# Strassen's seven products in the first MLP layer of three of four row blocks

## The chip, the core and the metric

The kernel runs on one core of a Trainium2 chip. The metric is the device time of one execution, in microseconds (us), as the median of several runs of the same program.

## The reference

The kernel mixes two branches over a sequence of 2048 rows of width 512, all in f32. The first is a linear attention with learned softmax features; the second is a two-layer MLP with a Mish between.

```python
g = sigmoid((x * gate_w).sum(-1, keepdims=True))
# a: 32 heads of 16; features = softmax(+-(head @ w_phi)), concatenated
qkv = x @ wqkv
phi_q, phi_k = features(q), features(k)
num = phi_q @ (phi_k.T @ v);  den = phi_q @ phi_k.sum(rows) + 1e-6
a = (num / den) @ wo
# b: hidden width 1376
h = x @ w1 + b1
b = (h * tanh(softplus(h))) @ w2
out = g * a + (1 - g) * b
```

## The kernel before, in words

Every f32 matmul that matters is done as three matmuls in the format `fp32r`: an operand is split into a high half (a rounded copy, made on ScalarE) and a low half (the difference, made on GpSimd or VectorE), and high·high, high·low and low·high are summed in PSUM.

The work has two stages. In the first, eight chunks of 256 rows go through the projections `k`, `v`, `q` and through the features of `k`; q goes out to DRAM (`pqd`), and the MLP's weights are loaded piece by piece (`ldw`) and split (`wh`, `wl`) one chunk later. The second stage has four row blocks of 512 rows. In a block:

- `up` i computes one tile of 128 hidden units for the 512 rows: 12 matmuls of 512 columns (three terms, four k tiles). `mi` is Mish on ScalarE, `hi` and `lo` are the two halves of its result (`lo`, variable `l`, on GpSimd). There are 11 tiles; the first holds 96 hidden units and, as an extra column, the gate.
- `dn` i adds that tile's part of the second layer into four PSUM banks (12 matmuls of 512 columns); the last one is `df0` to `df3`, one for each 128 rows.
- `lq`, `mx`, `mn`, `d0`, `d1`, `E`, `S`, `T`, `rS`, `D`, `m`, `de`, `rd`, `sc`, `es`, `tr` are the attention features of one tile of 128 rows: a load, then VectorE instructions, with an exponential on ScalarE (`E`). `tr` writes to DRAM (`ed`), `mv` loads it back transposed (`eT`).
- `nu`, `oh`, `ol`, `wo`, `ag`, `fi` are the attention's product, its split, the output projection, the gate, and the sum that is stored.
- `LX`, `XH`, `XL` load and split the next block's x (`xbh`, `xbl`).

No scheduler reorders anything: the order of instructions on every engine is that of strings written by hand (`BLOCK0`, `BLOCK1`, `BLOCK` twice), a word for each step; a word with `+` belongs to the next block, with `'` to the previous one. Each engine works through its queue in that order, and a step waits only for the semaphores of its operands and of the buffers that it reuses. Nearly all DMAs are issued from SP's queue, in the same order. All PSUM tiles of `up`, `num` and half of `wo` share three banks.

In a block before, the attention of the next block's first two tiles runs well ahead, up to `tr1+`, and no VectorE instruction of the MLP stands between `up` and `dn`.

Of the kernel before, what the change touches and what calls it, by code (L numbers as in the profile page):

```python
# [8 lines left out]
F32 = mybir.dt.float32  # L9
# [5 lines left out]
P = 128  # L15
# [16 lines left out]
ORDER = [NFA - 1] + list(range(NFA - 1)) + list(range(NFA, NF))  # L32
WARM = 10
# [10 lines left out]
    S1 rS1 ml1 z1 ve1 q0 qe0 st0 q1 qe1 st1  # L44
# [4 lines left out]
    S1 rS1 ml1 z1 ve1 q0 qe0 st0 q1 qe1 st1 mx0+ mn0+ kv" kv' kv  # L49
# [3 lines left out]
    S1 rS1 ml1 z1 v1 ve1 q0 mx1+ mn1+ d01+ d11+ qe0 st0 q1 qe1 st1 E1+  # L53
# [3 lines left out]
    v1 ve1 mx2+ mn2+ XL1 q0 qe0 st0 q1 qe1 st1 zt zf zs S0+ zl kv' kv rS0+ km  # L57
# [5 lines left out]
    up0 lq3 mi0 gr hi0 lo0 ldo0 ldo1 S1 rS1 up1 up2 mi1 hi1 lo1 wh0 wl0 d02 d12 T0 D0 m0 de0 rd0 sc0 es0 tr0 mi2 hi2 up3 dn0 hc lo2  # L63
    mi3 hi3 lo3 T1 D1 m1 de1 rd1 sc1 es1 tr1 mv0 lq0+ lq1+ mx3 mn3 d03 d13 WH0 dn1
    up4 mi4 hi4 lo4 WH1 WL0 dn2 E2 S2 T2 rS2 D2 m2 de2 rd2 sc2 es2 tr2 up5 mi5 hi5 lo5 WL1 dn3 E3 ge gg up6 mi6 hi6 lo6 dn4
    up7 mi7 hi7 lo7 dn5 S3 T3 rS3 D3 m3 de3 rd3 sc3 es3 tr3 mv1 up8 mi8 hi8 lo8 dn6
    mx0+ mn0+ d00+ d10+ mx1+ mn1+ d01+ d11+ lq2+ lq3+ up9 mi9 hi9 lo9 dn7 E0+ E1+ S0+ T0+ LX0 rS0+ D0+ m0+ de0+ rd0+ sc0+
    up10 mi10 hi10 lo10 dn8 dn9 cd nu0 nu1 oh0 ol0 es0+ tr0+ XH0+ XL0+ S1+ T1+ rS1+ LX1 df0 df1 wo0 ag0 wo1 oh1 ol1 ag1 D1+ fi0
    m1+ de1+ rd1+ sc1+ df2 df3 wo2 ag2 fi1 XH1+ XL1+ es1+ fi2 wo3 ag3 fi3 tr1+ mv0+
"""  # L70
BLOCK1 = """
    up0 mi0 hi0 lo0 gr mx2 mn2 d02 d12 mx3 mn3 d03 d13 up1 mi1 hi1 lo1 lq0+ lq1+ E2 E3 hc S2 T2 rS2 D2 m2 de2 rd2 sc2 es2 tr2
    up2 mi2 hi2 lo2 dn0 S3 T3 rS3 D3 m3 de3 rd3 sc3 es3 tr3 mv1 up3 mi3 hi3 lo3 dn1 up4 mi4 hi4 lo4 dn2
    mx0+ mn0+ d00+ d10+ mx1+ mn1+ d01+ d11+ lq2+ lq3+ up5 mi5 hi5 lo5 dn3 E0+ E1+ ge gg
    S0+ T0+ rS0+ D0+ m0+ de0+ rd0+ sc0+ es0+ tr0+ up6 mi6 hi6 lo6 dn4 up7 mi7 hi7 lo7 dn5 cd nu0 nu1 oh0 ol0 S1+ T1+ rS1+ D1+ LX0 LX1
    m1+ de1+ rd1+ sc1+ es1+ dn6 wo0 ag0 wo1 ag1 oh1 ol1 tr1+ mv0+ dn7 up8 mi8 hi8 lo8 mx2+ mn2+ d02+ d12+ mx3+ mn3+ d03+ d13+
    wo2 ag2 up9 mi9 hi9 lo9 dn8 E2+ E3+ up10 mi10 hi10 lo10 wo3 ag3 XH0+ XL0+ XH1+ XL1+ dn9 df0 fi0 df1 fi1 df2 fi2 df3 fi3
"""
BLOCK = """
    up0 mi0 hi0 lo0 gr lq0+ lq1+ S2 T2 rS2 D2 m2 de2 rd2 sc2 es2 tr2 up1 mi1 hi1 lo1 hc up2 mi2 hi2 lo2 dn0  # L80
    S3 T3 rS3 D3 m3 de3 rd3 sc3 es3 tr3 mv1 up3 mi3 hi3 lo3 dn1 up4 mi4 hi4 lo4 dn2
    mx0+ mn0+ d00+ d10+ mx1+ mn1+ d01+ d11+ lq2+ lq3+ up5 mi5 hi5 lo5 dn3 E0+ E1+ ge gg
    S0+ T0+ rS0+ D0+ m0+ de0+ rd0+ sc0+ up6 mi6 hi6 lo6 dn4 cd nu0 nu1 oh0 ol0 es0+ tr0+ S1+ T1+ rS1+ D1+ LX0 LX1 m1+ de1+ rd1+ sc1+
    es1+ dn5 wo0 ag0 wo1 ag1 oh1 ol1 tr1+ mv0+ dn6 up7 mi7 hi7 lo7 wo2 ag2 mx2+ mn2+ d02+ d12+ mx3+ mn3+ d03+ d13+
    up8 mi8 hi8 lo8 dn7 E2+ E3+ up9 mi9 hi9 lo9 wo3 ag3 up10 mi10 hi10 lo10 dn8 XH0+ XL0+ XH1+ XL1+ dn9 df0 fi0 df1 fi1 df2 fi2 df3 fi3
"""
# [3 lines left out]
def tile_gated_mix(ctx: ExitStack, tc: tile.TileContext, xT, wv, wkT, wqT, bd, w1a, w1b, b1, w2a, w2b, wo, out):  # L90
# [324 lines left out]

    def x_ops(b, load, split):

        raw = {}
        for h in range(2):
# [9 lines left out]
            def xl(h=h):  # L429
                sl = slice(h * SC, (h + 1) * SC)  # L430
                pin(V.tensor_sub(xb[b][1][:, :, sl], kt(raw[h], SC), f32(xb[b][0][:, :, sl])))  # L431
# [3 lines left out]
            at(split, f"XL{h}", xl)  # L435

# [75 lines left out]
    def b_ops(b):  # L512
        key = ("B", b)
        U, dn, eTs, num, ohl, io, ed = {}, {}, {}, {}, {}, {}, {}

        def up(i):
            f = ORDER[i]
# [78 lines left out]
        at(key, "gr", gr)  # L596
        at(key, "ge", ge)
# [3 lines left out]
        for t in range(4):  # L601
# [290 lines left out]
```

## Time and profile before

| | |
|---|---|
| runs | 444.29, 444.42, 444.49 us; median 444.42 |
| profiled execution | span 442.5 us, 1.9 us under the median of the runs |
| TensorE / VectorE / ScalarE / GpSimd busy | 437.8 / 313.2 / 201.4 / 159.6 us |
| projections and start | 0 to 149.35 us |
| row blocks 1 to 4 | 149.35 to 221.98, to 294.34, to 366.75, to 439.20 us |
| moved by DMA | 49.64 MB, 112 GB/s on average |

In the profile, PE is TensorE's matmuls and PEld its weight loads, which overlap; DVE is VectorE, ACT ScalarE, POOL GpSimd, SP the engine that issues most DMAs. The duration of a matmul row is its latency, 0.39 us for 512 columns; the pace is read from the starts of neighbouring rows. The same holds for VectorE rows, whose ends overlap the next start by up to 0.1 us.

### The profile page before, as it was taken

The page shows a single profiled execution, that of the slowest core. Times are in us where ns is not written, and L with a number is a line of the kernel's source. Part 1 is how long each engine was busy: PE and PEld are TensorE (multiplying, and loading weights), DVE is VectorE, ACT ScalarE, POOL GpSimd, SP SyncE. Part 2 cuts the span into 40 slices and gives each one's busy share as a digit, 9 for nine tenths or more (in the row PEclk, how much of TensorE's full clock was granted, in tenths as well). Part 3 has the DMA queues.
Part 4 walks back from the last instruction along what each step waited for, and adds up shares of the span by engine and source line. Part 5 has one row for each costly group of instructions (what it writes and reads, how often), then busy time and mean ns, then how long its engine had stood idle before and what let it go on. Part 6 is the DMA issues. An engine that isn't in the chain of part 4 may idle for free.

```text
span 442.5 us, 7179 instructions
## 1 busy us (share of the span) xinstructions
PE 437.8 (99%) x2874; PEld 359.9 (81%) x2874; DVE 313.2 (71%) x420; ACT 201.4 (46%) x286; POOL 159.6 (36%) x100
## 2 busy tenths in 40 slices
PE   8999999999999999999999999999999999999996
PEld 7888888888888888887888878888878888887885
DVE  3987739559699999999999898279679329601103
ACT  3644523533345455736376533646352645341330
POOL 3078694785662453621024120215310222411121
PEclk9999999999999999999999999999999999999999
DMA  7721631524403136425362533222605302310002
GB/s 265 283 96 48 191 120 50 188 86 133 167 29 116 49 84 209 142 101 168 128 205 96 159 124 120 75 96 95 191 0 192 94 2 96 134 57 1 0 0 96
DMA packets 29001, 49.64 MB, mean 112 GB/s; under 512 B 6308, under 2 KB 15012, under 8 KB 28968
## 3 DMA queue, kind: packets, MB, share of 16 engines
q1 hardware_dynamic: 28648, 48.79, 32.9%
q8 instruction: 22, 0.36, 0.3%
q10 hardware_dynamic: 288, 0.39, 0.3%
q14 instruction: 11, 0.09, 0.1%
q0 software_dynamic: 32, 0.01, 0.0%
HBM read 31.73 MB, written 16.79 MB: 110 GB/s over the span
## 4 chain that ended last, share of the span: by engine, by line
PE 98%; DMA 1%; SPq 0%; DVE 0%; issue 0%
PE proj L101 30%; PE up L101 27%; PE down L101 27%; PE wo L101 10%; PE kvp L101 2%; PE num L101 2%; DMA wT<-in_wkT_dram 1%; PE fuse L101 1%; PE rest L101 0%; DVE io L709 0%; SPq L157 0%; SPq L149 0%
## 5 line engine op out<-in xcount | busy, mean ns | idle before, releaser
L543 POOL TENSOR_TENSOR l<-act,h 128x512 fp32r<-128x512 f32 (+1 forms) x44 | 62.6, 1425 | 215.5 <-ACT h L121 192.7
L121 ACT ACTIVATE act<-up,b1s 128x512 f32<-128x512 f32 x44 | 30.3, 688 | 83.1 <-PE up L101 81.0
L330 POOL TENSOR_TENSOR zacc<-zacc,E 128x1024 f32<-128x1024 f32 x16 | 39.7, 2479 | 39.9 <-DVE E L287 31.4
L121 ACT ACTIVATE E<-E 128x1024 f32<-128x1024 f32 x32 | 33.5, 1060 | 36.0 <-DVE E L272 35.9
L287 DVE TENSOR_TENSOR E<-E,Sm 128x1024 f32<-128x1024 f32 x32 | 45.1, 1409 | 1.0
L101 PE MATMUL wo<-woh,ohl 128*128 128x512 f32 x128 | 41.2, 389 | 0.0
L276 DVE TENSOR_REDUCE Sm<-E 128x64 f32<-128x1024 f32 x32 | 38.5, 1204 | 0.0
L101 PE MATMUL down<-w2ah,h 128*128 128x512 f32 x96 | 37.6, 392 | 0.0
L101 PE MATMUL down<-w2al,h 128*128 128x512 f32 x80 | 31.2, 390 | 0.0
L101 PE MATMUL down<-w2ah,l 128*128 128x512 f32 x80 | 31.1, 389 | 0.0
L121 ACT ACTIVATE h<-act 128x512 fp32r<-128x512 f32 (+2 forms) x48 | 30.3, 632 | 1.6
L101 PE MATMUL down<-w2bh,h 128*128 128x512 f32 x78 | 30.6, 392 | 0.0
L101 PE MATMUL down<-w2bl,h 128*128 128x512 f32 x78 | 30.4, 389 | 0.0
L101 PE MATMUL down<-w2bh,l 128*128 128x512 f32 x78 | 30.4, 389 | 0.0
L431 DVE TENSOR_TENSOR xbl<-xraw,xbh 128x1024 fp32r<-128x1024 f32 x8 | 10.9, 1378 | 27.1 <-ACT xbh L121 27.1
L256 DVE TENSOR_REDUCE mx<-proj 128x32 f32<-128x512 f32 x16 | 11.0, 689 | 25.5 <-PE proj L101 25.5
L101 PEld LDWEIGHTS wo<-woh,ohl 128*128 128x128 f32 x128 | 24.0, 188 | 5.0
L121 ACT ACTIVATE io<-wo,g_sb 128x512 f32<-128x512 f32 x16 | 11.0, 690 | 36.0 <-PE wo L101 34.7
L121 ACT ACT_TABLE_LOAD x19 | 24.4, 1283 | 3.5 <-PE up L101 3.2
L101 PE MATMUL up<-xbh,w1ah 128*128 128x512 f32 x96 | 25.8, 390 | 0.0
L101 PE MATMUL up<-xbh,w1al 128*128 128x512 f32 x96 | 25.7, 389 | 0.0
L101 PE MATMUL up<-xbl,w1ah 128*128 128x512 f32 x96 | 25.7, 389 | 0.0
(125 smaller groups left out, 978.3 us busy)
## 6 DMA issues: line engine op xcount, KB each, us to landing
ed<-E SPq DMA_DIRECT2D x16, 512.0 KB, 2.9
eT<-ed SPq DMA_DIRECT2D x64, 128.0 KB, 3.2
xraw<-in_xT_dram SPq DMA_DIRECT2D x15, 512.0 KB, 4.3
pqd<-qs SPq DMA_DIRECT2D x16, 256.0 KB, 2.1
pq<-pqd SPq DMA_DIRECT2D x16, 256.0 KB, 3.8
out_dram<-io SPq DMA_DIRECT2D x15, 256.0 KB, 2.0
raw<-in_w1a_dram SPq DMA_DIRECT2D x3, 512.0 KB, 4.6
raw<-in_w2a_dram SPq DMA_DIRECT2D x3, 512.0 KB, 3.7
```

The costliest lines, as they stand in the source:

```text
L101: return pin(nc.tensor.matmul(*a, **k))
L121: return pin(A_.activation(out_, in_, fn, **k))
L256: pin(V.tensor_reduce(d[name], hv(src()), axis=AX.X, op=op))
L276: pin(V.tensor_reduce(d["S"], hv(d["E"][:, :]), axis=AX.X, op=ALU.add))
L287: pin(eng.tensor_mul(hv(d["E"][:, :]), hv(d["E"][:, :]), d["S"][:, :, None].to_broadcast([P, 2 * H, DH])))
L330: at(key, f"z{t}", lambda d=d: pin(G_.tensor_add(zacc, zacc, d["E"])))
L431: pin(V.tensor_sub(xb[b][1][:, :, sl], kt(raw[h], SC), f32(xb[b][0][:, :, sl])))
L543: pin(G_.tensor_sub(U[i]["l"][:n, :], U[i]["a"][:n, :], f32(U[i]["h"][:n, :])))
```

## The change

The eleven hidden tiles of a block are one gate tile and five pairs (tile g of the first 640 units and tile g of the last 640). For blocks 2, 3 and 4, each pair's first layer, a product of a 256x512 and a 512x512 matrix, is computed with Strassen's seven products of half the size instead of eight. A quarter of the operands is a slice of the weights or of x (`A11`, `B21`), the others are sums: `S1` to `S4` of the weights, `T1` to `T4` of x. Each product is six matmuls of 128x128 by 256 columns (three terms, two k tiles). Products accumulate in PSUM where the formula allows; the rest of the sums are three VectorE additions a pair (`a1`, `a2`, `a3`) of copies that ScalarE made (`c1`, `c2`).

What moves with it:

- The four weight sums are made in DRAM (`sums`): three copies on SP's queue in chunk 2 (`sc`), and accumulating DMAs from GpSimd's queue in chunks 3 to 5 (`sa`). In block 1 they are loaded (`ls`), split (`hs` on ScalarE, `os` on GpSimd, 128x1024 each, g = 0 to 3; the fifth falls into block 2) and stored with the unsummed quarters (`ts`, `tp`) as `prod`. In blocks 2 to 4 the seven weight operands of each pair come back in two transfers, `wA` (four operands, 8 KB a partition) and `wB` (three).
- The first-layer weights are kept by pairs, each piece loaded with two DMAs. The first block still uses them whole, with the old `up`.
- For the next block's x, four differences (`TT0` to `TT3`, VectorE, 128x512) and their halves (`TH` on ScalarE, `TL` on GpSimd, 128x1024 twice) are added, and `XL` moves from VectorE to GpSimd.
- `mv` is four DMAs instead of eight. The gate's load `gl` gets a place of its own. `df2'`, `fi2'`, `df3'`, `fi3'` finish a block at the head of the next. In blocks 3 and 4 all but `E` of the first two tiles is done in the block itself rather than in the one before.

The diff, cut:

```diff
+PAIRS = [NFA - 1] + [f for g in range(NFB) for f in (g, NFA + g)]
+UNITS = "A22", "A11", "A12", "S1", "S2", "S4", "S3"
...
 BLOCK0 = """
-    up0 lq3 mi0 gr hi0 lo0 ldo0 ldo1 S1 rS1 up1 up2 mi1 hi1 lo1 wh0 wl0 d02 d12 T0 D0 m0 de0 rd0 sc0 es0 tr0 mi2 hi2 up3 dn0 hc lo2
-    mi3 hi3 lo3 T1 D1 m1 de1 rd1 sc1 es1 tr1 mv0 lq0+ lq1+ mx3 mn3 d03 d13 WH0 dn1
...
-    mx0+ mn0+ d00+ d10+ mx1+ mn1+ d01+ d11+ lq2+ lq3+ up9 mi9 hi9 lo9 dn7 E0+ E1+ S0+ T0+ LX0 rS0+ D0+ m0+ de0+ rd0+ sc0+
-    up10 mi10 hi10 lo10 dn8 dn9 cd nu0 nu1 oh0 ol0 es0+ tr0+ XH0+ XL0+ S1+ T1+ rS1+ LX1 df0 df1 wo0 ag0 wo1 oh1 ol1 ag1 D1+ fi0
-    m1+ de1+ rd1+ sc1+ df2 df3 wo2 ag2 fi1 XH1+ XL1+ es1+ fi2 wo3 ag3 fi3 tr1+ mv0+
+    up0 lq3 mi0 gr gl hi0 lo0 ldo0 ldo1 S1 rS1 up1 up2 mi1 hi1 lo1 hs0 os0 wh0 wl0 d02 d12 T0 D0 m0 de0 rd0 sc0 es0 tr0 mi2 hi2 ts0 up3 dn0 hc lo2 hs1 os1
+    mi3 hi3 lo3 T1 D1 m1 de1 rd1 sc1 es1 tr1 ts1 mv0 lq0+ lq1+ mx3 mn3 d03 d13 WH0 dn1
...
+    up7 mi7 hi7 lo7 dn5 S3 T3 rS3 D3 m3 de3 rd3 sc3 es3 tr3 mv1 hs2 os2 up8 mi8 hi8 lo8 dn6
+    mx0+ mn0+ d00+ d10+ mx1+ mn1+ d01+ d11+ lq2+ lq3+ ts2 up9 mi9 hi9 lo9 dn7 E0+ E1+ S0+ T0+ LX0 rS0+ D0+ LX1 m0+ de0+ rd0+ sc0+
+    up10 mi10 hi10 lo10 dn8 dn9 cd nu0 nu1 ls3 wi oh0 XH0+ XH1+ XL0+ XL1+ ol0 TT0+ TT1+ TT2+ TT3+ es0+ tr0+ TH0+ TL0+ TH1+ TL1+ S1+ df0 df1 wo0 ag0
+    wo1 oh1 ol1 T1+ rS1+ ag1 D1+ fi0 m1+ de1+ rd1+ sc1+ hs3 os3 df2 wo2 ag2 fi1 es1+ wo3 ag3 ts3 tr1+ ls4+
 """
...
+def pairs(g, f3, f1, f2, f4=""):
+    n = g + 1
+    return f"""
+    s3_{g} wa_{g} a3_{g} {f3} s1_{n} c1_{n} s4_{g} wb_{n} M1_{g} a1_{n} {f1} H1_{g} L1_{g} {f4} dn{1 + 2 * g} s2_{n} c2_{n} a2_{n} M0_{n} H0_{n} L0_{n} {f2} dn{2 + 2 * g}
+    """
+
+def end(f3, last):
+    return f"""
+    s3_4 wa_4 a3_4 wo0 ag0 {f3} s4_4 wb_5 M1_4 H1_4 L1_4 dn9 XH0+ XH1+ XL0+ XL1+ TT0+ TT1+ TT2+ TT3+ wo1 ag1 TH0+ TL0+ nu1 oh1 ol1 TH1+ TL1+ {last} df0 df1 wo2 ag2 wo3 ag3 fi0 fi1
+    """
+
+BLOCK1 = (
+    """
+    up0 mi0 mx2 mn2 hi0 s1_0 wb_0 c1_0 gr a1_0 lo0 mv0 gl fi2' df3' fi3' d02 d12 s2_0 c2_0 a2_0 M0_0 H0_0 L0_0 mx3 mn3 hc dn0
+    """
+    + pairs(0, "d03 d13", "lq0+ lq1+ lq2+", "hs4 os4 S2 T2 rS2", "E2 E3 ge")
+    + pairs(1, "D2 m2 de2 rd2 sc2", "es2 tr2", "ts4 S3 T3 rS3 gg")
+    + pairs(2, "D3 m3 de3 rd3 sc3", "es3 tr3 mv1", "mx0+ mn0+ d00+ d10+ lq3+")
+    + pairs(3, "mx1+ mn1+ LX0 LX1", "d01+ d11+ mx2+ mn2+", "cd nu0 oh0 ol0 d02+ d12+")
+    + end("mx3+ mn3+ d03+ d13+", "E0+ E1+ E2+ E3+")
+)
+BLOCK2 = (
+    """
+    up0 mi0 S0 T0 s1_0 wb_0 c1_0 hi0 a1_0 lo0 gr df2' fi2' df3' fi3' gl s2_0 c2_0 a2_0 M0_0 H0_0 L0_0 hc rS0 D0 m0 de0 rd0 sc0 dn0
+    """
+    + pairs(0, "es0", "tr0 S1 T1", "rS1 D1 m1 de1 rd1 sc1 lq0+ lq1+ lq2+")
...
+    + end("mx1+ mn1+ d01+ d11+", "mx2+ mn2+ d02+ d12+ mx3+ mn3+ d03+ d13+ E0+ E1+ E2+ E3+")
+)
...
+            def os(d=d):
+                pin(G_.tensor_sub(d["l"], f32(d["l"]), f32(d["h"])))
...
+        names = UNITS[4:] if part else UNITS[:4] if G < last else UNITS[:1]
...
+        pin(Sy.dma_start(f32(t).rearrange("p x n e -> p x (n e)"), prod[G % NFB][:, :, o : o + n, :].rearrange("p x n e -> p x (n e)")))
...
-                pin(V.tensor_sub(xb[b][1][:, :, sl], kt(raw[h], SC), f32(xb[b][0][:, :, sl])))
+                pin((G_ if b else V).tensor_sub(xb[b][1][:, :, sl], kt(raw[h], SC), f32(xb[b][0][:, :, sl])))
...
+            def tl(j):
+                pin(G_.tensor_sub(raw["l"][:, pair(j)], raw["t"][:, pair(j)], f32(raw["h"][:, pair(j)])))
...
+            def add(ps, u, x, start=False):
+                (wh, wl), (xh, xl) = units[G, u], operand(x)
+                n = 0
+                for w, a in ((wh, xh), (wl, xh), (wh, xl)):
+                    for k in range(2):
+                        mm(ps, w[:, k * P : (k + 1) * P], a[:, k, :], start=(start and n == 0), stop=(n == 5), skip_group_check=True)
+                        n += 1
+
+            def s1():
+                d["b"] = psum("upb", "a")
+                add(d["b"][:, lo_], "S1", "T1", True)
+                add(d["b"][:, hi_], "A12", "B21")
+                d["a"] = psum("upa", "a")[:, lo_]
+                add(d["a"], "A11", "B11", True)
+
+            def s2():
+                add(d["a"], "S2", "T2")
+                add(d["b"][:, lo_], "S4", "B22")
...
+            def sum_(j, cs, ps):
+                o = d["A"][j][:, cs]
+                pin(V.tensor_add(o, ps, o))
```

275 lines of the change are left out of this document (217 added, 58 removed).

## The prediction

> **What bounds the kernel now.** I read the page first, then busy time by stage, then the single queues around the place where the change bites.
>
> ```profile
> span 442.5 us, 7179 instructions
> ...
> PE 437.8 (99%) x2874; PEld 359.9 (81%) x2874; DVE 313.2 (71%) x420; ACT 201.4 (46%) x286; POOL 159.6 (36%) x100
> ...
> PE 98%; DMA 1%; SPq 0%; DVE 0%; issue 0%
> ```
>
> TensorE is busy all the time and is 98% of the chain that ended last, so fewer matmul-microseconds shorten the run, but only as long as nothing makes TensorE wait. It has no slack to hide a wait in. The row blocks, in order (columns: stretch, its length, busy time of PE, PEld, DVE, ACT, POOL, clock, DMA share, GB/s):
>
> ```profile
> 149.35:221.98 72.63, 72.63 (x378) 59.30 (x378) 69.51 (x93) 38.42 (x53) 21.98 (x15) 1.00 0.41 131
> 221.98:294.34 72.36, 72.36 (x378) 59.12 (x377) 57.16 (x81) 38.96 (x53) 15.04 (x11) 1.00 0.35 117
> 294.34:366.75 72.41, 72.41 (x378) 59.11 (x377) 49.49 (x70) 33.58 (x48) 16.12 (x11) 1.00 0.31 104
> ```
>
> The clock is full throughout. The first row block is the one to look at: VectorE is busy 69.5 of 72.6 us there. It is a second bound, hidden only because nothing late in its queue is needed soon.
>
> **What is removed: matmul time.** In blocks 2 to 4 a pair of hidden tiles took 24 up matmuls of 512 columns and now takes 42 of 256 (seven products, three hi/lo terms, two k tiles). The last 26 wide matmuls and the 12 of `rest`, the only full-array ones of 256 columns, stand back to back (start, duration):
>
> ```profile
> 431.69 0.39 PE L101 MATMUL down<-w2bl,h 128*128 128x512 f32 x1
> ...
> 437.36 0.39 PE L101 MATMUL down<-w2bh,l 128*128 128x512 f32 x1
> 437.58 0.28 PE L101 MATMUL rest<-w2bh,h 128*128 128x256 f32 x1
> ...
> 438.90 0.28 PE L101 MATMUL rest<-w2bh,l 128*128 128x256 f32 x1
> ```
> ```profile
> 438.66 0.19 PEld L101 LDWEIGHTS rest<-w2bl,h 128*128 128x128 f32 x1
> 438.78 0.19 PEld L101 LDWEIGHTS rest<-w2bh,l 128*128 128x128 f32 x1
> ```
>
> Wide: (437.36 − 431.69)/25 = 0.2268 us a step. Half as wide: (438.90 − 437.58)/11 = 0.120 us, a little over half. The weight loads last 0.19 us but start 0.12 us apart, so they overlap and do not bind. A pair: 24 × 0.2268 = 5.44 us before, 42 × 0.120 = 5.04 us after; 0.40 us saved; fifteen pairs (three blocks of five): **6.05 us**. One eighth of the products is gone, but a fixed part of about 0.013 us per matmul is paid 42 times for 24. The Trainium skill (TensorE: Matmul & The Clock Gate, "Back-to-back issue gap") gives columns/2.4 plus 2.5 ns; by that the saving would be an estimated 8.9 us; the steps above contradict it at both widths, and the measured steps are used.
>
> **What a pair adds, in blocks 2 to 4.** Each pair adds three small VectorE sums (`a1`, `a2`, `a3`: PSUM plus SBUF, 128x256), three ScalarE copies and a split Mish. The nearest rows:
>
> ```profile
> L750 DVE TENSOR_TENSOR wkl<-fuse,wkh 128x256 fp32r<-128x256 f32 x8 | 2.8, 416 | 1.3 <-ACT wkh L121 1.3
> L121 ACT ACTIVATE wkh<-fuse 128x256 fp32r<-128x256 f32 x7 | 2.3, 387 | 6.1 <-PE fuse L101 6.1
> L543 POOL TENSOR_TENSOR l<-act,h 128x512 fp32r<-128x512 f32 x40 | 57.4, 1438 | 172.9 <-ACT h L121 150.1 <-issue 16.5 <-DMA eT<-ed 2.9
> L121 ACT ACTIVATE h<-act 128x512 fp32r<-128x512 f32 x40 | 25.3, 632 | 1.4
> ```
> ```profile
> 303.36 1.18 DVE L276 TENSOR_REDUCE Sm<-E 128x64 f32<-128x1024 f32 x1
> ...
> 310.81 0.65 DVE L256 TENSOR_REDUCE mx<-pq 128x32 f32<-128x512 f32 x1
> ```
>
> A pair now lasts 5.04 us plus two `down` groups of 12 × 0.2268, so 10.48 us of TensorE. VectorE has one attention tile a pair in block 3 (from the sum to the transpose, 310.81 − 303.36 = 7.45 us), and 3 × 0.42 = 1.3 us of sums: 8.7 of 10.48 us, so it keeps up. The new waits: `s4` needs `a3`, with the 18 matmuls of the next `s1` (2.16 us) between them, against about 0.2 us of matmul latency and 0.42 us: covered. The second half of `s2` needs `a1`: 0.72 + 2.72 + 0.72 us cover it. `dn` of the second tile needs Mish, `H1` (0.63) and `L1` (1.44), some 3 us, with `dn` and `s2` (4.2 us) between. I cost these at nothing in the steady pairs and 1.0 us in all for the seams into blocks 3 and 4, where ScalarE has four exponentials in front of `ag2`, `ag3` and `mi0` (bounds 0, and 2.5 us if the last exponential waits for a late `d13`).
>
> **Where the cover is missing: the end of block 1.** The diff puts eight new GpSimd subtractions of 128x1024 there: `os0` to `os3` (low halves of the summed weights) and `XL0`, `XL1`, `TL0`, `TL1` (low halves of the next block's x and of its four differences). What such a GpSimd instruction does to VectorE stands in this very block:
>
> ```profile
> 173.94 2.40 POOL L455 TENSOR_TENSOR wol<-raw,woh 128x1024 fp32r<-128x1024 f32 x1
> ...
> 180.87 2.40 POOL L455 TENSOR_TENSOR wol<-raw,woh 128x1024 fp32r<-128x1024 f32 x1
> ```
> ```profile
> 174.82 2.07 DVE L270 TENSOR_TENSOR E<-pq,mx 128x512 f32<-128x512 f32 x1
> 176.81 0.68 DVE L272 TENSOR_TENSOR E<-mn,pq 128x512 f32<-128x512 f32 x1
> 177.41 1.21 DVE L276 TENSOR_REDUCE Sm<-E 128x64 f32<-128x1024 f32 x1
> ...
> 181.32 2.03 DVE L634 TENSOR_TENSOR Dn<-Dn,Sm 128x64 f32<-128x64 f32 x1
> ...
> 192.16 0.27 DVE L634 TENSOR_TENSOR Dn<-Dn,Sm 128x64 f32<-128x64 f32 x1
> ```
>
> The subtraction at 174.82 took 2.07 us where its like takes 0.68, and ended 0.55 us after GpSimd's 2.40 us were over (176.34); the small product at 181.32 took 2.03 us where its like takes 0.27. VectorE stood still for 1.39 and 1.76 us. The Trainium skill (SBUF — State Buffer, "Who interferes with whom") says why: a VectorE instruction with two SBUF inputs and a GpSimd one that reads SBUF lock each other out for the whole instruction. The trace agrees: both victims have two SBUF inputs, and the reduction at 177.41, with one input, has its usual 1.2 us.
>
> Price of one added subtraction for VectorE: between 0 (it falls beside reductions and transposes) and its own 2.40 us; less than nothing is excluded, since a lock only delays. I take the smaller of the two rows, 1.39, as these two are alike in size and place: 8 × 1.39 = **11.1 us** of lateness. VectorE's end of the block, and TensorE's:
>
> ```profile
> 208.05 1.29 DVE L669 TENSOR_TENSOR ohl<-num,ohl 128x512 fp32r<-128x512 f32 x2 [0.82 <-ACT ohl L121]
> ...
> 211.67 1.18 DVE L431 TENSOR_TENSOR xbl<-xraw,xbh 128x1024 fp32r<-128x1024 f32 x1
> 212.77 1.21 DVE L276 TENSOR_REDUCE Sm<-E 128x64 f32<-128x1024 f32 x1
> ...
> 220.97 1.23 DVE L431 TENSOR_TENSOR xbl<-xraw,xbh 128x1024 fp32r<-128x1024 f32 x1 [0.80 <-ACT xbh L121]
> ...
> 223.25 1.40 DVE L714 SCALAR_TENSOR_TENSOR io<-down,og_sb,io 128x512 f32<-128x512 f32 x2
> ...
> 226.29 0.67 DVE L256 TENSOR_REDUCE mn<-pq 128x32 f32<-128x512 f32 x1
> 226.88 1.25 DVE L270 TENSOR_TENSOR E<-pq,mx 128x512 f32<-128x512 f32 x1
> ```
> ```profile
> 221.98 8.16 PE up L101 x36
> ```
>
> In the new order `a1_0` stands right behind `mn2`, at 226.88 in old times. Two `xbl` leave VectorE (2 × 1.10 us, by the starts at 211.67 and 212.77), two `fi` move behind `a1_0` (1.40), four differences `TT` come (4 × 0.60, by the starts at 176.81 and 177.41): 225.68. TensorE in the new order starts `up0` at 221.98 − 0.68 (`df3` moved behind) = 221.30; `up0` 2.72, `s1_0` 2.16, `df3` 0.68, half of `s2_0` 0.72: at 227.58 it needs `a1_0`, which takes 0.42 us. TensorE's steps are 12 and 3 of the wide kind, 18 and 6 of the narrow. Slack: 227.16 − 225.68 = 1.48 us, and VectorE's two idle gaps (0.82 and 0.80) are swallowed too: 3.10. What is late beyond that, TensorE waits, in `df0`, `wo2` (behind `ol1`) or `s2_0`: 11.1 − 3.1 = **8.0 us**. At the upper bound of the price it is 8 × 2.40 − 3.1 = 16.1 us.
>
> **The rest.** The summed weights are made in DRAM during the projections: three copies and ten stores on SP's queue, four accumulating transfers on GpSimd's, and each first-layer piece comes in two issues. GpSimd issued one transfer before:
>
> ```profile
> L186 POOL DMA_DIRECT2D b1s<-in_b_dram x1 | 0.7, 676 | 0.0
> ```
> ```profile
> xraw<-in_xT_dram SPq DMA_DIRECT2D x15, 512.0 KB, 4.3
> ```
> ```profile
> 114.56 32.86 PE proj L101 x144
> ```
>
> Four issues are 2.7 us on an engine with idle time a chunk ahead of its readers: nothing. No row shows an accumulating transfer; the other bound is that the second waits for the first's 2.6 MB (five times 4.3 us, some 21 us, against a chunk of the projections of about 17, the last row: two chunks), so 4 us of GpSimd time; I take 0, since a chunk of lead stands behind it. The operands: two transfers a pair, 1.0 and 0.8 MB. The larger one is issued after `s3` and needed at the `s1` one pair later, 10 us on; by the row above it lands in 4.3 to 8.6 us. Hidden.
>
> Sum: 442.5 − 6.05 + 8.0 + 1.0 = 445.5 us of span. The median of the runs, 444.42, lies 1.9 us above the profiled span; with the same 1.9 the forecast is **447.4 us**.
>
> **Rivals.** (1) The locks are cheap, faster. If a GpSimd subtraction delays VectorE by under 0.39 us (3.10/8), nothing waits: 444.42 − 6.05 = 438.4 us, 439.4 with the seams. Up to 1.0 us each (8.1/8) the change still gains. For it: some of the eight will fall beside reductions and transposes, which are not held up, and the new order moves work out of the block's end. Against: VectorE has no idle time to dodge into. (2) The operands come late. At 0.35 of the DMA engines' time now, 1.8 MB more a pair may double that; if the larger transfer took 12 us instead of under 10, each of fourteen pairs would wait 2 us: 447.4 + 28 = 475. Against, the first stretch of the kernel, where they moved 312 GB/s at a share of 0.88:
>
> ```profile
> 0.00:18.70 18.70, 17.29 (x313) 14.73 (x313) 11.62 (x24) 8.03 (x15) 3.37 (x12) 1.00 0.88 312
> ```
>
> (3) The weight loads bind at 0.19 us: 42 × 0.19 = 8.0 us a pair, 2.5 more than before, 444.4 + 38 = 482. Against: their starts 0.12 us apart. (4) The accumulating transfers hold GpSimd and with it the low halves of x: 4 us more, 451.
>
> **How the numbers follow.** A measurement of this kernel tells about 0.2% (0.9 us) from no change. Forecast (lock price above 1.0 us, or the seams dearer): 0.52, own range 445.3 to 455 (at 2.40 us a lock: 444.4 − 6.05 + 16.1 + 1.0 = 455.5). Rival 1: 0.33. Lock price near 1.0, within 0.2%: 0.06. Rivals 2, 3 and 4: 0.04, 0.02 and 0.03. So faster 0.33, same 0.06, slower 0.61. The range has to take in rival 1 and the dear locks: 438.2 to 455.
>
> **What would show it.** Right: block 1's stretch longer by about 8 us while blocks 2 to 4 are shorter by about 2 us each; VectorE rows with two SBUF inputs at 2 us or more beside `ss`, `xbl` and `xtl` on GpSimd; TensorE idle before `df0`, `wo` or `upb`, put down to VectorE or to ScalarE and GpSimd behind it; 256-column steps of 0.12 us. Wrong: no idle TensorE in block 1 (rival 1); TensorE waiting for `wA` or `wB` (rival 2); steps of 0.19 us (rival 3); idle time in the projections (rival 4).

## The result: 461.07 us, 3.9% slower, and where the time went

The changed kernel takes 461.07 us (five runs, 460.70 to 464.13) against 444.42 (444.29 to 444.75) for the kernel before: ratio 1.039, 95% interval 1.036 to 1.042. The forecast was 447.4, range 438.2 to 455.0: slower was right, the size was not. The first of the runs (464.13 us) is the profiled one; its page begins (busy time, then the chain that ended last by engine):

```profile
span 462.4 us, 7984 instructions
...
PE 443.3 (96%) x3144; PEld 371.7 (80%) x3144; DVE 354.1 (77%) x471; ACT 228.5 (49%) x355; POOL 206.6 (45%) x121
...
PE 35%; DVE 22%; DMA 6%; ACT 4%; issue 2%; SPq 0%; POOL 0%; DVEq 0%; ACTq 0%
```

TensorE was 98% of the chain; now it is 35%, and VectorE 22%. TensorE's busy time did not fall, it grew from 437.8 to 443.3 us. By row blocks (the columns are those of the prediction's windows):

```profile
149.85:237.94 88.09, 78.02 (x379) 61.07 (x374) 81.22 (x95) 44.13 (x59) 45.27 (x23) 0.94 0.59 197
237.94:308.88 70.94, 70.77 (x465) 61.00 (x463) 51.93 (x79) 41.70 (x71) 27.96 (x16) 1.00 0.76 267
308.88:385.96 77.08, 73.13 (x467) 62.78 (x466) 58.19 (x83) 42.00 (x70) 24.16 (x15) 0.98 0.64 209
385.96:459.20 73.24, 72.81 (x479) 63.03 (x477) 48.37 (x73) 35.11 (x64) 14.21 (x11) 1.00 0.53 169
```

Block 1, in which no product changed, is 88.09 us instead of 72.63; block 2 is 1.4 us shorter; block 3 is 4.7 us longer; block 4 is 0.8 us longer. (On the old footing block 1 lost `df3` to block 2 and block 2 `df2` and `df3` to block 3, 0.68 us each, and so on: block 2 really saves 0.74 us, block 4 some 0.6.) TensorE's waits of over 3 us in these blocks, in a timeline of PE (start, duration; in brackets the wait before it and its releaser; `ohl` holds the halves of the attention's product, made by `oh` and `ol`), with the steps behind one of them:

```profile
213.22 0.59 PE L134 MATMUL num<-eT,kvb 64*32 64x256 f32 x2 [3.25 <-DMA eT<-ed]
...
229.66 0.79 PE L134 MATMUL wo<-woh,ohl 128*128 128x512 f32 x1 [4.36 <-ACT ohl L154]
230.25 0.63 PE L134 MATMUL wo<-wol,ohl 128*128 128x512 f32 x1
230.68 0.63 PE L134 MATMUL wo<-woh,ohl 128*128 128x512 f32 x1
...
378.80 0.80 PE L134 MATMUL wo<-woh,ohl 128*128 128x512 f32 x1 [3.53 <-ACT ohl L154]
```

After the wait for `ohl` the steps of 512 columns are 0.43 us apart, not 0.227, and the clock column (third from the end) of a window over them says why: TensorE was granted half its clock.

```profile
230.25:235.37 5.12, 5.12 (x13) 3.96 (x12) 5.12 (x6) 1.55 (x3) 5.12 (x3) 0.50 0.26 106
```

That lasts until 235.4 at the first of these places (12 steps in 5.1 us instead of 2.7), until 382.3 at the second. The Trainium skill (TensorE: Matmul & The Clock Gate, "Part 1: The HAM clock gate") says that the clock falls to a half after an idle window of about 3.4 us and comes back after about as long of busy time; these rows agree in size (waits of 3.25 to 4.36 us, half clock for 3.4 to 5.7 us), and a row below shows it after a shorter wait.

Why `wo2` waits for ScalarE at 229.66, from the timelines of the three engines:

```profile
220.50 5.19 POOL L567 TENSOR_TENSOR xbl<-xraw,xbh 128x1024 fp32r<-128x1024 f32 x2 [6.04 <-ACT xbh L154]
220.78 2.68 DVE L584 TENSOR_TENSOR xt<-xraw,xraw 128x512 f32<-128x512 f32 x1 [0.83 <-DMA xraw<-in_xT_dram]
223.49 2.76 DVE L588 SCALAR_TENSOR_TENSOR xt<-xt,xraw 128x512 f32<-128x512 f32 x1
226.17 0.68 DVE L586 TENSOR_TENSOR xt<-xraw 128x512 f32<-128x512 f32 x1
226.28 2.26 ACT L154 ACTIVATE xth<-xt 128x1024 fp32r<-128x1024 f32 x2 [4.59 <-DVE xt L588]
228.45 0.67 ACT L154 ACTIVATE io<-wo,g_sb 128x512 f32<-128x512 f32 x1
229.02 1.07 ACT L154 ACTIVATE ohl<-num 128x512 fp32r<-128x512 f32 x2
```

The next block's x lands at 220.6. VectorE's first two differences (`TT`) stand still while GpSimd makes `XL`, 2.7 us each where the third takes 0.68. ScalarE waits 4.59 us for them in `TH`, and `ag0` and `oh1`, whose inputs had long been there, stand behind `TH` in its queue. The load itself is late, 7.7 us to its landing where it took 4.3 before (medians of all 15 loads of x, in the page's DMA issues; the first one at this place took 7.7 too):

```profile
xraw<-in_xT_dram SPq DMA_DIRECT2D x15, 512.0 KB, 7.7
```

And VectorE is late because GpSimd's subtractions lock it, as forecast: the same product `E` x `Sm` beside `os0` and, eleven microseconds on, beside nothing (timelines of GpSimd and VectorE):

```profile
164.43 2.40 POOL L493 TENSOR_TENSOR ss<-ss 128x1024 fp32r<-128x1024 f32 x1 [5.51 <-ACT ss L154]
164.59 3.32 DVE L320 TENSOR_TENSOR E<-E,Sm 128x1024 f32<-128x1024 f32 x1
175.61 1.23 DVE L320 TENSOR_TENSOR E<-E,Sm 128x1024 f32<-128x1024 f32 x1
```

### The profile page after: what moved, and what is told of

Same layout as the page of the kernel before. It is cut to its first block, busy times and chain, and to the rows that moved or that the text cites. A ratio compares the mean times of both kernels' runs of the same rounds, so it can differ in the third digit from the quotient of the medians.

```text
span 462.4 us, 7984 instructions
## 1 busy us (share of the span) xinstructions
PE 443.3 (96%) x3144; PEld 371.7 (80%) x3144; DVE 354.1 (77%) x471; ACT 228.5 (49%) x355; POOL 206.6 (45%) x121
## 3 DMA queue, kind: packets, MB, share of 16 engines
q0 software_dynamic: 1248, 4.59, 5.2%
## 4 chain that ended last, share of the span: by engine, by line
PE 35%; DVE 22%; DMA 6%; ACT 4%; issue 2%; SPq 0%; POOL 0%; DVEq 0%; ACTq 0%
PE down L134 15%; PE upa L134 7%; PE wo L134 7%; PE upb L134 5%; DMA xraw<-in_xT_dram 3%; DVE E L320 2%; DVE T L873 2%; DVE Dn L877 2%; DVE E L303 2%; DVE Sm L309 1%; DVE xt L588 1%; DMA ed<-E 1%; PE up L134 1%; DVE xt L584 1%; DVE E L888 1%
## 5 line engine op out<-in xcount | busy, mean ns | idle before, releaser
L806 POOL TENSOR_TENSOR l<-act,h 128x512 fp32r<-128x512 f32 x30 | 40.8, 1359 | 121.0 <-ACT h L154 84.7
L134 PE MATMUL wo<-woh,ohl 128*128 128x512 f32 x128 | 44.7, 417 | 8.1 <-ACT ohl L154 7.9
L320 DVE TENSOR_TENSOR E<-E,Sm 128x1024 f32<-128x1024 f32 x32 | 48.9, 1530 | 0.7
L716 POOL TENSOR_TENSOR l<-act,h 128x512 fp32r<-128x512 f32 (+1 forms) x14 | 19.4, 1392 | 45.0 <-ACT h L154 20.3
L787 DVE TENSOR_TENSOR act<-upb,act 128x256 f32<-128x256 f32 x30 | 12.6, 421 | 28.1 <-ACT act L154 18.9
L281 POOL TENSOR_TENSOR xl<-xraw,xh 128x512 fp32r<-128x512 f32 x14 | 20.4, 1601 | 18.6 <-ACT xh L154 18.6
L931 DVE TENSOR_TENSOR ohl<-num,ohl 128x512 fp32r<-128x512 f32 x16 | 10.4, 686 | 21.7 <-ACT ohl L154 18.7
L134 PE MATMUL wo<-wol,ohl 128*128 128x512 f32 x64 | 26.8, 419 | 0.0
L154 ACT ACTIVATE qs<-proj 128x512 f32<-128x512 f32 x16 | 9.6, 599 | 33.4 <-PE proj L134 29.1
L154 ACT ACTIVATE act<-act,b1s 128x512 f32<-128x512 f32 (+1 forms) x30 | 18.4, 614 | 13.9 <-DVE act L787 13.8
```

The source lines that it names most:

```text
L134: return pin(nc.tensor.matmul(*a, **k))
L154: return pin(A_.activation(out_, in_, fn, **k))
L281: pin(eng.tensor_sub(xs[c][1][j], kt(rawx[c], SC)[:, 2 * j : 2 * j + 2, :], f32(xs[c][0][j])))
L320: pin(eng.tensor_mul(hv(d["E"][:, :]), hv(d["E"][:, :]), d["S"][:, :, None].to_broadcast([P, 2 * H, DH])))
L716: pin(G_.tensor_sub(U[i]["l"][:n, :], U[i]["a"][:n, :], f32(U[i]["h"][:n, :])))
L787: pin(V.tensor_add(o, ps, o))
```

## Experiments

Theories: A, ScalarE's in-order queue holds back `oh1`, `ag2`, `ag3` behind work that waits; B, VectorE is late by the locks (a GpSimd subtraction during which a VectorE instruction with two SBUF inputs stands still); C, the added transfers make loads late; D, the halved clock costs time of its own. All edits are against the changed kernel unless it is said otherwise. Medians of four or more runs; the kernel before, run beside them, was at 444.4 to 444.8.

**The changed kernel again.**

> The changed kernel as it is, for comparison on the same chip: 460.5 to 464 us, waits of 3.3 us before num and of 4.4 and 3.5 us before wo2.

Measured 462.68 us (460.99 to 463.49). The profiled execution (timelines of VectorE and TensorE) shows how much the same program varies: the last transpose before `num` ended 5 us earlier than in the first profile, and `num` (from 207.8) hardly waited, against the 3.3 us expected, while the wait before `wo2` was about the same.

```profile
198.29 1.25 DVE L888 STREAM_TRANSPOSE E<-E 128x1024 f32<-128x1024 f32 x1
...
209.55 1.09 PE L134 MATMUL num<-eT,kvb 64*32 64x256 f32 x30 [0.26 <-ACT act L154]
...
225.66 0.80 PE L134 MATMUL wo<-woh,ohl 128*128 128x512 f32 x1 [4.73 <-ACT ohl L154]
```

In the first profile that transpose stands at 203.29. Block 1 is 83.7 us here, 88.1 there. So the wait before `num` comes and goes with the places where the locks fall (the product `E` x `Sm` that took 3.32 us in the first profile took 2.22 here, and others grew); a difference of up to some 4 us in block 1 between two single profiles means nothing by itself.

**e1_late_x: `TT`, `TH`, `TL` behind `oh1` and `ol1`.**

```diff
-XL1+ TT0+ TT1+ TT2+ TT3+ wo1 ag1 TH0+ TL0+ nu1 oh1 ol1 TH1+ TL1+
+XL1+ wo1 ag1 nu1 oh1 ol1 TT0+ TT1+ TT2+ TT3+ TH0+ TL0+ TH1+ TL1+
```

> The four differences of the next block's x (TT) and their halves (TH, TL) stand behind oh1 and ol1, at the ends of blocks 1, 2 and 3. Theory A (ScalarE's queue: the copies TH wait for late differences and hold back ag0 and oh1, for which wo2 waits): the idle time before wo2 (4.36 and 3.53 us in the changed kernel) falls under 1 us, the slow steps behind it (2.8 and 1.7 us) go too: 461.1 - 12.4 = 448.7, with up to 2 us given back in s1 of the next block, 448 to 451 us. Theory B (VectorE is late by the locks, as the prediction had it): the wait only moves, to ol1 or to the first sum: 459 to 462 us. Theory C (the load of x lands late, whatever the order): the wait moves to up0 or s1 of the next block: 456 to 460 us.

Measured 462.82 us, just above what B allowed. Block 1 fell to 77.1 us and the waits before `wo2` went, as A says; but two new waits of the same size came, as B says (timeline of PE):

```profile
237.90 0.81 PE L134 MATMUL upb<-xbh,wB 128*128 128x256 f32 x4 [4.48 <-DVE act L787]
...
386.52 1.22 PE L134 MATMUL upa<-xbh,wA 128*128 128x256 f32 x4 [4.26 <-ACT io L154]
```

The first is the sum `a1` of block 2, behind an attention tile of which two small products took 2.0 and 2.3 us beside `xtl` and `ss`. The second is `ag3`, behind `E2` and `E3` in ScalarE's queue, which waited for the attention's differences (`d12`, 2.89 us instead of 0.68) locked by `xtl`. With the slow steps behind them they took back all that block 1 had gained.

**e2_wi_late: the first three operand loads 12 us later.**

```diff
-nu1 ls3 wi oh0
+nu1 ls3 oh0 ... tr0+ wi
```

> The three operand loads for the first pairs (2.8 MB) are issued behind the store of the first transposed tile of block 2, some 12 us later, instead of right behind the load of the next block's x. Theory C (those loads fill the DMA queues, so that x lands in 7.5 us instead of 4.3): x lands 3 us sooner, the idle time before the first wo2 falls from 4.36 to about 1.4 us, its slow steps go: 455 to 456.5 us. If x is late by the stores ahead of it, or is not what wo2 waits for: landing 7 to 8 us, 460 to 462 us.

Measured 466.50 us, above both expectations. x landed no sooner: issued from 211.36, it took 8.5 us, and ScalarE's second copy of it waited until 221.08 although no operand load ran. The operands then came late themselves (TensorE waited 0.57 for `wB` and 1.91 us for `wA`). So C is wrong for these loads at this place.

**e3_lx_early and e7_seam: the seams of blocks 3 and 4.**

```diff
-pairs(3, "es3", "tr3 mv1 mx0+ mn0+ LX0 LX1", ...)
+pairs(3, "es3 LX0 LX1", "tr3 mv1 mx0+ mn0+", ...)
```

> In block 3 the two loads of the next x are issued one pair part earlier, ahead of the store of the last transposed tile and of the reading back (they stand there in block 2's list). Theory A: the idle time of 3.53 us before wo2 at the end of block 3 and the 1.7 us of slow steps go, block 1's end is unchanged: 455.5 to 456.5 us. Theory B: no change, 460 to 462 us.

Measured 458.59 us, between the two expectations: the wait of 3.5 us before `wo2` went; 1.77 us in front of block 4 came (`ag3` behind `E3`). e7 moves `E2` and `E3` into the next block's first pair as well.

> Seams into blocks 3 and 4 only: the early loads of x in block 3 as in the run before, and in blocks 3 and 4 the exponentials E2 and E3 of the block's own tiles move from the end of the block before into its first pair, so that ag2 and ag3 (which free PSUM banks) no longer stand behind them in ScalarE's queue. Theory A (ScalarE's order): the 1.8 us of wait before the first product of block 4 that the early loads left goes, block 4 from 74.6 to 72.5 us, block 3 71.7 as there: 458.6 - 2.0 = 456.6 us (456 to 457.5). If two more table switches in the first pairs hold up the Mish steps: 458.5 to 460 us.

Measured 455.82 us, ratio 1.025 (1.023 to 1.027); block 3 in the windows of e7:

```profile
305.58:377.25 71.67, 71.25 (x467) 61.64 (x466) 52.93 (x79) 44.26 (x72) 23.28 (x15) 1.00 0.68 224
```

A holds for the seams: 5.3 us of the loss were two places of order.

**e6_no_ops: 28 of 31 operand loads left out** (the expectation counts 26 of 29).

> Left out: 26 of the 29 operand loads (23 MB); all pairs compute with the first pair's weights, products and order stay. Theory C (the operand stream fills the DMA queues and makes the loads of x, the reading back and with them the waits late): the load of x in block 3 lands in 4 to 5 us instead of 7.7, the wait of 3.5 us there shrinks to about 1, 457 to 458 us; block 1's end, where only three operand loads are issued, stays as it is. If the transfers are not late by the operands: 460.5 to 462 us.

Measured 457.99 us. Block 3 was 71.67 us and its wait before `wo2` gone, block 1 stayed at 85.9. But x's own landing in block 3 fell only from 7.0 to 7.7 us to 6.2 to 6.9, not to the 4 to 5 expected. What changed more is its issue, 2.8 us sooner in the block: the reading back that stands ahead of it in SP's queue waited 2.2 us for its store instead of 5.2. So the operand stream made x late in block 3 (C), mostly through SP's queue, and not in block 1; e3 shows that order alone mends it.

**e4_hot and e12_hot_wo2: TensorE's waits filled with zeros.**

```diff
+        mm(dn[3], zero, wob["l"][:, :512], start=False, stop=False)   # 18 or 14 times, ahead of wo2
```

> Matmuls with a weight tile of zeros, which add nothing, fill TensorE's idle time: 13 ahead of num and 18 ahead of wo2 in block 1, 14 ahead of wo2 in block 3. All waits stay as they are. Theory D (each wait of over 3 us makes TensorE run at half its clock for some us after it): wo2 starts where it started, its steps are 0.23 us instead of 0.43: 2.8 + 1.7 = 4.5 us less, 456 to 457.5 us; the gain behind num is hidden by the wait for ohl. If the slow steps come from something else (supply of data, the load on the memory): steps stay 0.43, 460 to 462 us.

Measured 466.04 us. The steps behind `wo2` were 0.23 us as expected, but the 13 fillers before `num` waited 3.83 us themselves, for the tile of zeros from GpSimd, and ended late (`num` at 215.88 instead of 213.22), so the time says nothing. The cleaner run:

> As e4_hot, without the 13 filling matmuls before num: only the waits before wo2 at the ends of blocks 1 and 3 are filled (18 and 14 matmuls with zeros). If the slow steps behind a wait are on the path: wo2 starts where it starts in the unchanged run beside it, blocks 1 and 3 are 2.8 and 1.7 us shorter and the total is 3 to 4.5 us below that run. If VectorE and the transfers decide what comes after: the same steps at 0.23 us, but a new wait behind them, total within 1.5 us of the unchanged run.

Measured 460.20 us (459.59 to 462.38), 2.5 below the unchanged kernel beside it (460.99 to 463.49). Its timeline of PE:

```profile
225.54 0.50 PE L134 MATMUL wo<-woh,ohl 128*128 128x512 f32 x1 [0.41 <-ACT ohl L154]
225.87 0.39 PE L134 MATMUL wo<-wol,ohl 128*128 128x512 f32 x1
...
253.48 0.74 PE L134 MATMUL upb<-xth,wA 128*128 128x256 f32 x4 [1.28 <-DMA wA<-prod]
```

`wo2` starts at 225.54, in the unchanged kernel at 225.66; its steps are 0.23 us; block 2 begins 1.7 us sooner, and 1.28 us of that goes to a wait for operands. D is real, but only a part of the expected 3 to 4.5 us came off the total: 2.5 us by the medians, whose runs overlap, and 1.1 us by the two profiles, where new waits in block 4 (0.54 and 0.76 us) took some more.

**e5_no_os and e11_os_dve: the subtractions of the summed weights left out, or moved to VectorE.**

```diff
-pin(G_.tensor_sub(d["l"], f32(d["l"]), f32(d["h"])))      # e5: left out
+pin(V.tensor_sub(d["l"], f32(d["l"]), f32(d["h"])))       # e11
```

> Left out: the five GpSimd subtractions os0 to os4 that make the low halves of the summed weights (their unsplit sums are used in place of them); transfers, copies and order stay. Theory B (each of them locks VectorE out for 1 to 2 us, and VectorE's lateness decides when num can start): os0, os1 and os2 stand before num, the wait for lo2 behind os0 (1.6 us) goes, num starts 5 to 7 us sooner, 454 to 456 us. If the reading back of the transposed tiles (DMA) decides instead: num within 2 us of where it was, 459 to 461 us.

Measured 458.99 us, 2.1 below the changed kernel's first median and 3.7 below its second. `num` started at 209.0, but the unchanged kernel's did so at 207.8 once, so the 4 us at `num` prove nothing, and block 1 was 83.7 us, as in the unchanged kernel's second profile; the wait at the second tile's low half behind `os0` (0.7 to 2.6 us in most other profiles of this order) went.

> One thing changed against the changed kernel: os0 to os4 run on VectorE instead of GpSimd; same order, same transfers. Lock theory: VectorE gives 1.2 us of its own for each instead of 2.1 us of standing still, and lo2 no longer waits behind os0 on GpSimd (1.6 us): num starts 2 to 3 us sooner, 457.5 to 459 us. If the lock is not the cause: VectorE is later by 1.2 us a piece, 463 to 465 us.

Measured 469.19 us, a miss of both: on VectorE the subtractions wait for ScalarE's high halves, which wait for the loads of the sums (4.1 and 3.3 us, in the view of waits), and all attention stands behind them.

```profile
DVE ss L493 <- ACT ss L154: 4.1, 1, 4.1
DVE sl L493 <- ACT sh L154: 3.3, 1, 3.3
```

**e8_no_sums: loads, splits and stores of the summed weights left out.**

> The changed kernel without the work on summed weights in block 1 and early block 2: their loads (ls), high halves (hs, ScalarE), low halves (os, GpSimd) and stores (ts) are left out; two more stores a group during the projections fill their places with unsummed weights. The differences of x, products, operand loads and order stay. Theory B (the weight preparation's locks and transfers make VectorE and the reading back late): block 1 loses at least the 4.2 us that num came sooner without os, the wait of 4.4 us before wo2 shrinks since x lands in 5 us, 450 to 454 us. If the differences of x and ScalarE's order alone make block 1 long: block 1 still over 83 us, 457 to 459 us.

Measured 453.49 us. Block 1, in the windows of e8:

```profile
150.10:225.81 75.71, 72.74 (x380) 58.32 (x374) 72.45 (x90) 40.24 (x55) 33.58 (x19) 1.00 0.48 157
```

It is 75.7 us with the same order, where the unchanged kernel had 88.1 and 83.7 in its two profiles: most of what it had gained in length is this preparation, its locks and its transfers together.

**v1, v2: block 1 in another order, seams as in e7.** Core of v1 (v2 moves the third pair's sums behind `num` and lets block 2 take one attention tile a pair):

```diff
-    ... es3 tr3 mv1 hs2 os2 up8 ...
+    ... es3 LX0 LX1 tr3 mv1 hs2 os2 up8 ...
-    up0 mi0 mx2 mn2 hi0 s1_0 wb_0 c1_0 gr a1_0 lo0 mv0 gl ...
+    up0 mi0 hi0 s1_0 wb_0 c1_0 gr a1_0 lo0 gl fi2' df3' fi3' S1 T1 rS1 ...
```

> The seams as in e7, and block 1 put in another order: summed weights' halves behind the low half that the second layer waits for, the next x loaded ahead of the last transposed tile, its copies and differences done as soon as it lands, block 2's first attention tile behind the differences and its second one moved into block 2, and the first sum of block 2 ahead of both. Theory A and B together (VectorE's lateness by locks and the order of the queues, no new cost of the products): block 1 falls from 88.1 to 75 to 77 us, blocks 2 to 4 stay at 71, 71.7 and 72.5: 445 to 448 us. If the added operations themselves fill VectorE whatever the order: block 2 becomes longer than 74 us, 450 to 455 us.

Measured 456.53 us, above both expectations. Block 1 fell to 79.8, no further: `num` waited 3.24 us, and block 2 rose to 77.1 (a wait of 3.13 us for `a3` behind the attention tile moved there).

> The order of v1, and: the summed weights of the third pair no longer before num but behind it (then the fourth's and the fifth's follow one slot later), block 2 with one attention tile a pair as in blocks 3 and 4, the first sum ahead of the attention tile at each block's start and the tile's small products behind the third sum. Theory A and B together: num no longer waits behind the lock of os2 (2.1 us) and oh0 not for the store of the third pair's weights, so block 1 falls from 79.8 to 74 to 76 us; block 2 from 77.1 to 71.5; 444.5 to 447.5 us. If the load on the memory keeps the reading back late (7 us instead of 3 to 4): block 1 stays over 78 us, 449 us or more.

Measured 460.89 us. Block 1 79.2; block 2 81.2, since the fifth pair's operands, whose sums came one slot later, were waited for (timeline of PE in v2):

```profile
279.54 1.22 PE L134 MATMUL upb<-xth,wA 128*128 128x256 f32 x4 [7.32 <-DMA wA<-prod]
```

**e9_v2_no_sums: the order of v2 without the preparation.**

> The order of v2 without the work on summed weights in blocks 1 and 2 (left out as in the run above). This is the floor of the products themselves: block 1 as before (72.5 to 73 us), blocks 2 to 4 shorter by 0.7 each: 441.5 to 443 us. The difference to v2 is the price of the preparation in the best order tried. If it stays above 444.5, the products bring nothing even when their preparation is free.

Measured 443.62 us, ratio 0.9981 (0.9971 to 0.9991), a little above the range expected. Blocks 1 to 3 in its windows:

```profile
149.62:222.33 72.71, 72.22 (x381) 58.49 (x374) 63.89 (x81) 40.04 (x55) 32.63 (x19) 1.00 0.48 156
222.33:292.94 70.61, 70.61 (x465) 60.97 (x464) 55.85 (x86) 40.37 (x69) 24.37 (x15) 1.00 0.70 235
292.94:364.86 71.92, 71.48 (x468) 61.45 (x467) 58.55 (x87) 44.14 (x72) 23.29 (x15) 1.00 0.69 231
```

Its longest wait in block 3, in the timeline of PE:

```profile
302.17 0.50 PE L134 MATMUL down<-w2ah,h 128*128 128x512 f32 x1 [0.44 <-DVE io L974]
```

All operand loads run, no wait of the four blocks is over 0.5 us, the clock is full: this is what the products are worth in this order with that preparation free (the sums in DRAM and the differences of x are still made), 1.0 us of 444.6.

**v3, v3a, v3b: lock or transfers?** v3 is v2 with the fifth pair's sums earlier; v3a puts `os0` and `os1` on VectorE, where they now stand behind landed loads; v3b has no subtraction, the low halves come from accumulating transfers.

> The order of v2, but the fifth pair's summed weights are loaded some 12 us earlier, into the buffers of the third's, so that the fifth pair's operands don't come late (a wait of 7.3 us, and its slow steps, in v2). Block 2 from 81.2 to 71.5 to 72 us, block 1 stays at 79: 451 to 452.5 us. If the operands are still late: 455 us or more.

> As v3, with the first two pairs' subtractions (os0, os1) on VectorE (1.2 us each by its rows of this size) instead of GpSimd. Lock theory: each GpSimd subtraction cost VectorE 2.1 us, so the last transposed tile is ready some 1.8 us sooner, num's wait falls from 3.2 to 1.4 us, and with a wait that short the slow steps behind it go too: 446 to 449 us. Transfer theory: VectorE gains nothing that shows, since the reading back lands when the memory lets it: 451 to 453 us.

> As v3, without any subtraction: ScalarE writes the high half and then its negative over the sum, and an accumulating transfer adds that to a copy of the sum which was stored during the projections; the low half so comes out of the transfer. 2.6 MB more of copies, five more issues on GpSimd (1.4 us each), no lock by os. Lock theory: the last transposed tile 4 us sooner, no wait before num, block 1 at 73 to 74 us: 444.5 to 446.5 us. Transfer theory: the added transfers make the reading back later: 452 to 456 us.

Measured 457.87, 456.61 and 459.01 us; block 1 in the windows of v3 and then of v3a:

```profile
149.85:229.28 79.43, 74.98 (x380) 59.38 (x374) 67.91 (x84) 42.96 (x58) 39.12 (x22) 0.96 0.58 189
```
```profile
149.33:223.96 74.63, 73.30 (x380) 58.44 (x374) 66.30 (x82) 42.75 (x58) 35.97 (x20) 1.00 0.62 202
```

Block 1 was 4.8 us shorter with two of the locks taken away. VectorE was busy 66.30 us there instead of 67.91, although it now did the two subtractions itself (2.32 us); the wait before `num` fell from 2.89 and 1.35 us to 0.78, and the clock stayed full. A single pair of profiles would not show this, since the unchanged kernel's two differ by 4.4 us in block 1. What speaks for the locks is that v1, v2 and v3 agree (79.8, 79.2, 79.4), and so do v3a and v4 below, both with these two on VectorE (74.6, 75.8). v3b's block 1 lies between (77.9).

v3a and v3b missed both of their expectations, because in none of the three did block 2 come down (79.3, 83.5, 80.5 us). TensorE waited for `a3`: 2.96 and 3.27 us in v3 and v3a, behind small attention products, one of which took 1.91 us instead of 0.23 beside `os4`, and 1.21 us in v3b, which has no such subtraction. And it waited for `wA` (2.35, 4.96, and twice in v3b, 2.61 and 2.34), whose load stood in SP's queue behind a reading back that waited 9.7 to 10.0 us for its store.

**v4: all subtractions on VectorE, block 2's order mended** (the cut of the diff is against v3a).

```diff
-    + pairs(2, "es2", "tr2 S3 T3", "rS3 D3 m3 de3 rd3 sc3")
+    + pairs(2, "D2 m2 de2 rd2 sc2 mv0 es2", "tr2 S3 T3", "rS3")
```

> As v3a, with all five subtractions on VectorE, and in block 2 the tile's small products behind the third sum of a pair, and the reading back of the first tiles behind the operand load of the fifth pair in SP's queue. If only order was left: block 1 74.6 us as there, block 2 from 83.5 to 71.5 to 72.5, blocks 3 and 4 as in v3a: 445 to 447 us, level with or up to half a per cent above the kernel before. If the transfers themselves are the limit in block 2 (loads, stores and operands together): 450 us or more.

Measured 450.25 us (448.63 to 452.45), ratio 1.0135 (1.011 to 1.016): the best order found with the whole computation, at the lower edge of the second expectation (450 or more), and still slower than the kernel before. Blocks 1 and 2 in its windows:

```profile
149.41:225.22 75.81, 74.13 (x379) 59.75 (x374) 65.65 (x87) 42.98 (x58) 31.94 (x19) 0.98 0.61 198
225.22:298.26 73.04, 71.04 (x465) 61.01 (x463) 55.40 (x84) 42.14 (x71) 25.42 (x15) 1.00 0.84 285
```

Against e9 that is 3.1 us more in block 1 and 2.4 in block 2; blocks 3 and 4 are level. The waits left are 1.68 us before `num`, for the reading back, with slow steps behind it, and 1.52 us in block 2 for `a3`, which stood behind `os4` on VectorE. So the transfers are not shown to be the limit in block 2.

## Why the prediction was right and wrong

Slower was right, and two steps of the sum failed. In the profiled executions block 1 grew by 15.5 us where 8.0 were forecast, and blocks 2 to 4 grew by 4.0 together where they were to shrink by 5.05 (6.05 saved, 1.0 for the seams, the passages from one block to the next).

The account, in medians: the products alone −1.0 us (e9 against the kernel before); the preparation in the best order tried +6.6 (v4 against e9); the order in which the change places it, and the engine of its subtractions, +10.8 (461.07 against 450.25), of which the seams 5.3 (e7). With the changed kernel's second median, 462.68, the last two are 12.4 and 6.9.

- **"6.05 us saved": mis-sized.** The pace was right: a pair starts every 10.5 us as computed, 329.61 to 340.13 in the trace after:

```profile
329.61 0.64 PE L134 MATMUL upa<-xth,wB 128*128 128x256 f32 x4
...
340.13 0.64 PE L134 MATMUL upa<-xth,wB 128*128 128x256 f32 x4
```

  But a block saves 0.74 us (block 2), not 2.02. The working counted matmuls at their steps and gave the new order no price. In block 3 of e9 it has one: at 0.2267 and 0.120 us a step its matmuls make 70.2 us and it lasts 71.9, where the old block lost 0.2. Half of the 1.7 us is in `dn0`, whose PSUM banks the moved `fi2` and `fi3` still hold; the rest is `num` in two halves, and 0.03 us each time that a second-layer group follows narrow matmuls (2.75 us instead of 2.72).
- **"Steady pairs cost nothing, seams 1.0": half right.** The steady pairs wait for nothing over 0.5 us. The seams cost 5.3 us: ScalarE's queue was looked at for its four exponentials only, and a late load of x (7.0 to 7.7 us to its landing, issued behind a reading back) had no price.
- **"8 x 1.39 = 11.1 us of lateness, 8.0 us of wait at the end of block 1": mechanism right, place and size wrong.** The locks are there, 2.1 us on `E`, 2.0 on two of the four `TT` at the ends of blocks 1 and 3 (none at the end of block 2), and without two of them block 1 of v3a was 4.8 us shorter than v3's. But TensorE did not wait in `df0`, for `ol1` or in the first `s2`. In the first profile it waited for `num`'s input, in the second hardly; in both it waited for `oh1` in ScalarE's queue, where `TH` had been placed ahead of it. The forecast followed VectorE's queue and never walked ScalarE's. TensorE stood idle for 10.1 and 8.2 us of block 1 in the two profiles; that this is near 8.0 is luck, since the waits are others. One reading under this term did not show what it was taken for: beside the reduction at 177.41 no GpSimd instruction ran (the next began at 179.22). The reduction at 174.23 would have shown it, 0.67 us as usual beside the subtraction of 173.94.
- **The halved clock: left out.** In the changed kernel the slow steps behind a long wait took up to 2.8 us more. By e12 those behind the two waits before `wo2` were worth 1.1 us (profiles) to 2.5 us (medians) of the total.
- **"Transfers 0": right for the operands in steady pairs, wrong for what shares the queues with them.** `wA` lands in 5.8 us as bounded; the load of x took 7.7.
- **Rivals.** Cheap locks: wrong. Late operands: not in the changed order, but in e2, e12, v2, v3 and its variants. Weight loads at 0.19 us: wrong, steps are 0.12. Accumulating transfers: the projections ended at 149.85 and 149.37 in the two profiles, against 149.35: nothing that shows.

Open: how the 6.6 us between v4 and e9 divide into locks and transfers, and whether a better order would get them back. The best that any order here left, with the preparation free, is 1.0 us; e9's own order still loses 1.7 us in block 3, so that is no proof of a limit.

## What to carry to other kernels

An algebraic saving is worth its matmul time at most, and only in a stage where the other engines and queues have slack for its preparation; here 6 us of arithmetic, of which 1 us was left in the best case, needed operands whose making cost block 1 some 8 to 12 us (e8 against the two profiles of the changed kernel). When steps are placed into an in-order queue, walk each engine's queue and ask what stands behind a step if its input is late: the most expensive waits here were finished work standing behind unfinished. Price a wait of TensorE at more than its length.

## What was not expected of the hardware

TensorE's steps of 512 columns go from 0.227 to 0.43 us after a wait, for some 3 to 6 us. Waits of 3.3, 3.5 and 4.4 us did it; in e3 one of 2.63 did, while 1.62 us in the changed kernel did not. The length alone does not decide: 2.84 us in e11 and 2.76 us in e8 left the granted clock at 1.00, while 2.02 us in e6 and 1.68 us in v4 were followed by 0.50. The timeline of PE in e3:

```profile
170.85 0.50 PE L134 MATMUL down<-w2ah,l 128*128 128x512 f32 x1 [2.63 <-POOL l L716]
...
171.90 0.63 PE L134 MATMUL down<-w2ah,l 128*128 128x512 f32 x1
172.32 0.63 PE L134 MATMUL down<-w2ah,h 128*128 128x512 f32 x1
```

So the 3.4 us of the Trainium skill's page named above is no safe allowance. And a program that hides nothing any more varies more: the kernel before stayed within 0.5 us in the five runs beside the changed one and within 1.8 in every other set, the changed one within 3.4, v4 within 3.8.
